# Lightning attention and a Mish layer by seven products: one bank opened earlier, three steps moved up, one sum on GpSimd

## The chip, the cores and the metric

The kernel runs on one core of a Trainium2 chip. The metric is device time in microseconds (us) for one execution. A profile shows one execution: its span is the time from the first to the last instruction, and its own time adds what lies around the span.

## The reference

Two parts, one after the other. First a causal attention with decay: 4 batches, 8 heads, 768 positions, head size 64, with `lam` one decay per head. The reference works in blocks and carries a state:

```
out   = ((q k^T) * D) v + (q * lam^(i+1)) state
state = lam^block * state + (k * lam^(block-1-i))^T v
```

Its output, seen as x of 3072 rows by 512, goes through two matrix products with an activation between them: `h = x @ w_in` (512 to 2048), `g = h * tanh(softplus(h))` (Mish), `out = g @ w_out` (2048 to 512). Inputs and output are float32; the kernel computes in float16 with float32 sums.

## The kernel before

**Tiling.** The positions are cut into six groups (n = 0 to 5) of 128 positions of each of the four batches, so a group has four chunks of 128 tokens, 512 tokens in all, and 24 chunks run through the kernel (group n has chunks 4n to 4n+3). While TensorE does the two layers of group n, the attention of group n+1 is done in between, and the loads of group n+2 are issued. The first layer gives hidden features in 16 tiles of 128; `hsg` holds Mish of them, `xt` the tokens that come in.

**Seven products.** The second layer is computed for 2x2 blocks of tokens and features by seven products instead of eight (P1 to P7, `fast_unit` from L660), which needs sums of quarters of `w_out` (`tsum`, `weight_sum` L452) and of `hsg` (`gsum`, `token_sum` L571). In groups 2 to 5 the last four of the 16 hidden tiles of the first layer are computed in the same way (`set_unit` L506), from sums of `w_in` (`isum`, `in_sum` L472) and of `xt` (`xsum`, `x_sum` L484). There the order is P1, P2, P5, P6, P7, P3, P4. P1 is copied out (`u1`), P2 adds to it in its bank and goes to Mish. P5 is copied to `p5`. P6 adds to P1: ScalarE copies `u1` into the bank of z (L546), and P6's products add to that; ScalarE then copies z into the bank of y (L561). P7 adds to z, P3 to y, and VectorE adds `p5` to both (L542) for Mish.

**Order.** The schedule is written out by hand: each engine runs its instructions in the order in which the program issues them, and waits by semaphores. A list of units (L733 for group 0, L797 for the others) is what TensorE does; after each unit the loop issues what is attached to its number: loads (`slots`, on GpSimd's queue, behind a small `pace` copy), sums, `turn` (scales k, L269, and transposes q and k by DMA on SyncE's queue), and `visit` (attention). In groups 2 to 5, where `d` is 2, units 0 to 3 and 6 to 9 are each two hidden tiles for half of the tokens (`mm1_duo` L422, eight products), unit 4 is P1 and such a tile pair, unit 5 P2 and one, unit 10 P5 and P6, unit 11 a tile pair, unit 12 P7 and P3, unit 13 a tile pair and P4; units 14 to 27 are the second layer.

**Attention in the visits.** `pair_a` (L320) forms k^T v of two chunks (`pv`, L328) in two PSUM banks; VectorE adds the state (`raw`, L288) and scales it (`state`, L293). `pair_s` (L338) forms the scores of two chunks in four banks (L349), the part from the state (L357), and masks the scores on VectorE (`sb`, L365). `pair_o` (L368) applies them to v, scales the result and transposes it into the next `xt`. In group 0 the attention of group 1 goes chunk by chunk: `look_t` (transposes of k and q, `pk` and `pq`, L211), `look_s` (scores, masks L239), `look_kv` and `look_o`. It needs each chunk's scaled k (`ktil`, `scale_k` L262), which VectorE makes, and GpSimd for chunks 6 and 7 (L265).

**Banks.** PSUM has eight banks, given out by tags: `ph` two, `po` two, `pS`, `pk`, `pq`, `pO` one each. A tile with a tag waits until the readers of the tile before in that bank are done. In `set_unit` the tags are set at L532: x (P1, P2) and z (P6, P7, P4) in `po`, w (P5) in `pS`, y (P3) in `pk`. In unit 5 `pair_a` takes both `po` banks; in unit 6 `pair_s` takes `pS`, `pk` and both `po` banks.

**In group 0** units 0 to 15 are the hidden tiles one by one (`mm1_unit` L410), 16 to 19 P1 and P5, 20 to 23 P6 and P2 in halves, 24 to 29 P7, P3, P4. `in_sum` is issued after unit 12, ahead of the `weight_sum` and `token_sum` steps that P5 and P6 read. `weight_sum(3, 1)`, the second half of the sum that P4 reads, is issued after unit 25 on VectorE.

Of the kernel before, what the change touches and what calls it, by code (L numbers as in the profile page):

```python
# [20 lines left out]
def kernel(  # L21
# [10 lines left out]
    nc = tc.nc  # L32
# [7 lines left out]
    NKI = DF // 128  # L40
# [228 lines left out]
    def turn(i):  # L269

        scale_k(i)
        for src, name, to in ((qn, "qraw", qraw), (ktil, "kraw", kraw)):
            to[i] = work.tile([128, JP, C], F16, name=name, tag=name, bufs=4)
            nc.sync.dma_start_transpose(out=to[i], in_=src[i].rearrange("p h c -> p (h c)"))
# [171 lines left out]
    tsum = [const.tile([128, HK, HN], F16, name=f"tsum{i}") for i in range(4)]  # L446
# [2 lines left out]

        return wout[2 * r + s][:, :, c * HN : (c + 1) * HN]  # L450

    def weight_sum(i, s):  # L452

        ks = slice(s * NKI // WS, (s + 1) * NKI // WS)
        a, b, op = (
            (w_quarter(0, 1, s), w_quarter(0, 0, s), ALU.subtract),
            (w_quarter(1, 1, s), tsum[0][:, ks, :], ALU.subtract),
            (w_quarter(1, 1, s), w_quarter(0, 1, s), ALU.subtract),
            (w_quarter(1, 0, s), tsum[1][:, ks, :], ALU.subtract),
        )[i]  # L460
        nc.vector.tensor_tensor(out=tsum[i][:, ks, :], in0=a, in1=b, op=op)  # L461

    KH = NKC // 2
    SU = NKI - 4
# [19 lines left out]
    def x_sum(n, i):  # L484

        xsum[n, i] = work.tile([128, KH, 2 * C], F16, name=f"xsum{i}", tag=f"xsum{i}", bufs=1)
        x = xt[n]
        k0_, k1_ = slice(0, KH), slice(KH, NKC)
        lo, hi = slice(0, 2 * C), slice(2 * C, 4 * C)
        a, b, op = (  # L490
            lambda: (x[:, k0_, hi], x[:, k1_, hi], ALU.add),
            lambda: (xsum[n, 0], x[:, k0_, lo], ALU.subtract),
            lambda: (x[:, k0_, lo], x[:, k0_, hi], ALU.subtract),
            lambda: (x[:, k1_, lo], xsum[n, 1], ALU.subtract),
        )[i]()
        nc.vector.tensor_tensor(out=xsum[n, i], in0=a, in1=b, op=op)
# [9 lines left out]
    def set_unit(n, step):  # L506

        def x_quarter(r, c):
            return lambda kk: xt[n][:, c * KH + kk, r * 2 * C : (r + 1) * 2 * C]

        def x_part(i):
            return lambda kk: xsum[n, i][:, kk, :]

        def w_quarter_(r, c):
            return lambda kk, m: i_quarter(r, c)[:, kk, m * 128 : (m + 1) * 128]

        def w_part_(i):
            return lambda kk, m: isum[i][:, kk, m * 128 : (m + 1) * 128]

        key, lhs, rhs = {  # L520
            "P1": lambda: ("x", w_quarter_(0, 0), x_quarter(0, 0)),
            "P2": lambda: ("x", w_quarter_(1, 0), x_quarter(0, 1)),
            "P6": lambda: ("z", w_part_(1), x_part(1)),
            "P5": lambda: ("w", w_part_(0), x_part(0)),
            "P7": lambda: ("z", w_part_(2), x_part(2)),
            "P3": lambda: ("y", w_quarter_(1, 1), x_part(3)),
            "P4": lambda: ("z", w_part_(3), x_quarter(1, 1)),
        }[step]()

        def place(key):  # L530
            if (n, key) not in first:
                tag, bufs = {"x": ("po", 2), "z": ("po", 2), "w": ("pS", 1), "y": ("pk", 1)}[key]  # L532
                first[n, key] = ps.tile([128, 2, 2 * C], F32, name=f"s{key}", tag=tag, bufs=bufs)
            return first[n, key]

        def kept(key, src, tag, bufs):
            first[n, key] = work.tile([128, 2, 2 * C], F32, name=key, tag=tag, bufs=bufs)
            nc.scalar.activation(first[n, key], src, AF.Copy)  # L538

        def plus_(r, key):  # L540
            o = work.tile([128, 2, 2 * C], F32, name="hs", tag="hs", bufs=2)
            nc.vector.tensor_tensor(out=o, in0=first[n, key], in1=first[n, "p5"], op=ALU.add)  # L542
            return lambda: mish(n, r, 1, o)

        if step == "P6":
            nc.scalar.activation(place("z"), first[n, "u1"], AF.Copy)  # L546
        t = place(key)
        for m in range(2):
            for kk in range(KH):
                nc.tensor.matmul(  # L550
                    t[:, m, :], lhs(kk, m), rhs(kk),
                    start=(step in ("P1", "P5") and m == 0 and kk == 0), stop=(kk == KH - 1),
                    skip_group_check=True)
        if step == "P1":
            kept("u1", t, "osb", 4)
        elif step == "P2":
            mish(n, 0, 0, t)
        elif step == "P5":
            kept("p5", t, "p5", 1)
        elif step == "P6":  # L560
            nc.scalar.activation(place("y"), t, AF.Copy)  # L561
        elif step == "P7":
            plus_(1, "z")()
        elif step == "P3":
            plus_(0, "y")()
        elif step == "P4":
            mish(n, 1, 0, t)
# [165 lines left out]
    units = [(mm1_unit, (0, ni)) for ni in range(NKI)]  # L733
# [4 lines left out]
    for u, (fn, args) in enumerate(units):  # L738
        put_off = []
        fn(*args, **({"then": put_off} if u in (23, 25) else {}))  # L740
        if u < B - 1:
            look_kv(u + 1, "pq" if u == 0 else "po")()
        if 8 <= u < 8 + NVB - B:
            nc.vector.memset(vz[u - 8 + B][:, :, D : 2 * D], 0.0)
        elif u == 13:
            nc.vector.tensor_scalar(out=maskT, in0=rel, scalar1=0.0, scalar2=None, op0=ALU.is_ge)
        for i, s in {14: ((0, 0),), 15: ((0, 1),), 18: ((1, 0), (2, 0)),
                     20: ((1, 1), (2, 1))}.get(u, ()):
            weight_sum(i, s)
        for i, part in sums.get(u, ()):  # L750
            token_sum(0, i, part)
        if u == NKI - 4:
            for i in range(4):
                in_sum(i)
        if u == 22:
            scale_k(4)
            weight_sum(3, 0)
        then = [f(i, "po" if i == 5 else "ph") if f is look_kv else f(i) for f, i in visit.get(u, ())]
        if u == 23:
            scale_k(5)  # L760
            scale_k(6)
        if u == 25:
            weight_sum(3, 1)
        for f in put_off + then:
            if f:
                f()
        if u in (25, 26, 27):
            for _ in range(2):
                ahead.pop(0)()
        if u == 26:  # L770
            scale_k(7)
    next_state(1, 0)

    for n in range(1, NG):
        r, s, t = Pair(), Pair(), Pair()
        r.n, r.bs, s.n, s.bs, t.n, t.bs = n, (2, 3), n + 1, (0, 1), n + 1, (2, 3)
        visit = {}
        d = 0 if n == 1 else 2
        if 1 < n < NG - 1:
            visit[5] = pair_a, r  # L780
        if n < NG - 1:
            visit[6 if d else 11] = pair_s, s
            visit[16 - d] = pair_o, s
# [7 lines left out]
        def duo(g, half):  # L791
            return mm1_duo, (n, g, half * (GT // 2), (half + 1) * (GT // 2))

        def part(step):
            return set_unit, (n, step)

        if d:  # L797
            units = [[duo(g, 0)] for g in range(4)]
            units += [[part("P1"), duo(4, 0)], [part("P2"), duo(5, 0)]]
            units += [[duo(g, 1)] for g in range(4)]  # L800
            units += [[part("P5"), part("P6")], [duo(4, 1)], [part("P7"), part("P3")], [duo(5, 1), part("P4")]]
        else:
            units = [[duo(g, half)] for half in range(2) for g in range(NKI // 2)]
# [14 lines left out]
        for u, calls in enumerate(units):  # L818
            for fn, args in calls:
                fn(*args)  # L820
            if n == 1 and u == 0:
                turn(8)
                look_s(7)
            if n == 1 and u == 2:
                f = look_kv(7)
                look_o(7)
                f()
                next_state(1, 1)
            for _ in range({0: 1, 1: 1, 2: 2, 3: 1, 4: 1}.get(u, 0) if n == 1 else 0):
                pace()  # L830
                ahead.pop(0)()
            if later and u in slots:
                pace()
                later.pop(0)()
            for i, part in sums.get(u, ()):
                token_sum(n, i, part)
            if turns.get(u, NG * B) < NG * B:
                turn(turns[u])
            if u in visit:
                f, s_ = visit[u]  # L840
                s_.spare = ("po", "po") if u < 12 else ("pS", "pk") if f is pair_a else ("ph", "po")
                f(s_)
            if d and u in (6, 8):
                for i in (0, 1) if u == 6 else (2, 3):
                    x_sum(n, i)


# [28 lines left out]
```

## Time and profile before

| | |
|---|---|
| Median of 3 runs | 210.1 us (209.75 to 210.49) |
| Profiled execution, its own time | 209.93 us |
| Its span | 208.2 us |
| Granted TensorE clock, mean | 1.000 |
| VectorE busy | 142.6 us (69%) |
| ScalarE busy | 98.9 us (48%) |
| GpSimd busy | 81.1 us (39%) |

How to read the lines that follow: PE is TensorE (PEld its weight loads), DVE VectorE, ACT ScalarE, POOL GpSimd, SP SyncE; a q behind the name is that engine's queue of instructions. A line names the source line (L550), the operation, and out<-in by the names of the tiles. In the timeline the first two numbers are start and length in us; in brackets stands how long the engine was idle before, and what released it. Products overlap each other, so a length includes the time that a product takes to pass through; the distance between two starts is the better measure. A wait for several semaphores is put down to the one that came last.

### The profile page before, as it was taken

Reading aid. Unit: us, or ns where it says so; the run is one execution under the profiler, and the core shown is the slowest. Engines: PE = TensorE matmul, PEld = TensorE weight load, DVE = VectorE, ACT = ScalarE, POOL = GpSimd, SP = SyncE. Lnnn points to the kernel's source line nnn. Section 1 sums busy time; section 2 is a strip of 40 time slices with the busy share of each in tenths; the row PEclk is TensorE's granted clock in tenths of the full one; section 3 lists DMA queues with packets and bytes.
Section 4 is the critical chain, followed back from the end, with each engine's and each line's share of the span. In section 5 each row is a group of like instructions: output and inputs, shape, how many; then the busy total and the mean of one; then the engine's idle time right before and its main releaser. Section 6 shows DMA issues by size and latency. Waiting matters only on the chain. (4 is left out here: it accounts for less than half of the span.)

```text
span 208.2 us, 5077 instructions
## 1 busy us (share of the span) xinstructions
PE 193.2 (93%) x2065; PEld 158.9 (76%) x2065; DVE 142.6 (69%) x279; ACT 98.9 (48%) x174; POOL 81.1 (39%) x129
## 2 busy tenths in 40 slices
PE   7978998999999999997999997999997999997993
PEld 3645445878888998875998875998875988886883
DVE  7788369799927969384799574799565676322823
ACT  5684663323665421746530646530646630676430
POOL 7994333795678950037751027752000000000000
PEclk9999999999999999999999999999999999999999
DMA  9999999999999999849999759999950023500014
GB/s 131 144 148 197 207 205 188 155 182 201 141 122 181 153 128 231 206 80 92 89 136 214 182 102 82 93 116 211 208 104 8 2 50 104 151 3 0 3 50 153
DMA packets 112459, 26.82 MB, mean 129 GB/s; under 512 B 101555, under 2 KB 112435, under 8 KB 112435
## 3 DMA queue, kind: packets, MB, share of 16 engines
q0 software_dynamic: 77552, 13.37, 88.7%
q1 hardware_dynamic: 30848, 9.97, 26.3%
q10 hardware_dynamic: 4034, 3.15, 5.0%
q8 instruction: 16, 0.26, 0.5%
q14 instruction: 9, 0.07, 0.1%
HBM read 27.26 MB, written 6.29 MB: 161 GB/s over the span
## 5 line engine op out<-in xcount | busy, mean ns | idle before, releaser
L434 PE MATMUL ph<-xt,win 128*128 128x256 f16 x512 | 60.9, 273 | 0.0
L434 PEld LDWEIGHTS <-win 128*128 128x128 f16 x512 | 49.1, 98 | 5.9
L441 ACT ACTIVATE hsg<-ph 128x512 f16<-128x512 f32 x64 | 38.1, 596 | 24.9 <-PE ph L434 24.8
L600 PEld LDWEIGHTS <-gsum 128*128 128x128 f16 x384 | 36.5, 98 | 6.8 <-DVE gsum L586 1.1
L600 PEld LDWEIGHTS <-hsg 128*128 128x128 f16 x272 | 26.0, 98 | 3.3
L586 DVE TENSOR_TENSOR gsum<-hsg 128x1024 f16<-128x1024 f16 x24 | 15.8, 687 | 12.9 <-ACT hsg L441 7.6
L600 PE MATMUL z<-tsum,gsum 128*128 128x256 f16 x192 | 23.3, 273 | 0.6 <-DVE tsum L461 0.6
L600 PE MATMUL x<-wout,hsg 128*128 128x256 f16 x192 | 23.7, 273 | 0.0
L75 POOL DMA_DIRECT2D qn<-in_q_dram x23 | 20.4, 888 | 7.6 <-DMA wout<-in_moe_w_out_dram 3.3
L67 POOL DMA_DIRECT2D kn<-in_k_dram x23 | 20.5, 892 | 6.1 <-DMA win<-in_moe_w_in_dram 2.4
L78 POOL DMA_DIRECT2D vz<-in_v_dram x24 | 21.2, 884 | 4.1 <-DMA wout<-in_moe_w_out_dram 1.7
L396 POOL COPY paced<-hsg 1x1 f16<-1x1 f16 x33 | 8.9, 270 | 34.8 <-ACT hsg L441 33.8
L365 DVE TENSOR_TENSOR sb<-pS,maskT 128x512 f16<-128x512 f32 x32 | 19.9, 682 | 0.9 <-PE pS L349 0.7
L288 DVE TENSOR_TENSOR raw<-pv,state 64x256 f32<-64x256 f32 x24 | 10.1, 422 | 13.5 <-PE pv L328 12.9
L265 DVE TENSOR_TENSOR ktil<-kn,lk 128x512 f16<-128x512 f16 (+1 forms) x22 | 14.6, 684 | 2.4 <-DMA kn<-in_k_dram 2.4
L405 PE MATMUL ph<-xt,win 128*128 128x512 f16 x64 | 14.5, 379 | 0.3 <-ACT xt L257 0.3
L657 ACT ACTIVATE osum<-z 128x512 f32<-128x512 f32 x5 | 3.0, 598 | 23.7 <-PE z L600 23.7
L542 DVE TENSOR_TENSOR hs<-sz,p 128x512 f32<-128x512 f32 x4 | 2.8, 692 | 15.5 <-PE sz L550 15.5
L600 PE MATMUL w<-tsum,gsum 128*128 128x256 f16 x96 | 11.8, 273 | 0.6 <-DVE gsum L586 0.6
L600 PE MATMUL y<-wout,gsum 128*128 128x256 f16 x96 | 12.3, 273 | 0.0
L417 ACT ACTIVATE hsg<-ph 128x512 f16<-128x512 f32 x16 | 9.6, 597 | 5.8 <-PE ph L405 5.8
L550 PEld LDWEIGHTS <-isum 128*128 128x128 f16 x64 | 6.2, 96 | 7.4 <-issue 6.2
(114 smaller groups left out, 271.8 us busy)
## 6 DMA issues: line engine op xcount, KB each, us to landing
vz<-in_v_dram POOLq DMA_DIRECT2D x24, 128.0 KB, 5.5
out_dram<-osum SPq DMA_DIRECT2D x12, 256.0 KB, 3.6
kn<-in_k_dram POOLq DMA_DIRECT2D x23, 128.0 KB, 5.4
qn<-in_q_dram POOLq DMA_DIRECT2D x23, 128.0 KB, 5.3
out_dram<-osum ACTq DMA_DIRECT2D x11, 256.0 KB, 3.9
wout<-in_moe_w_out_dram POOLq DMA_DIRECT2D x4, 512.0 KB, 16.7
win<-in_moe_w_in_dram POOLq DMA_DIRECT2D x3, 512.0 KB, 10.2
win<-in_moe_w_in_dram POOLq DMA_DIRECT2D x2, 256.0 KB, 6.3
```

The lines of the kernel that those rows point to most:

```text
L67: nc.gpsimd.dma_start(out=kn[i], in_=chunk_rows(k, i))
L75: nc.gpsimd.dma_start(out=qn[i], in_=chunk_rows(q, i))
L78: nc.gpsimd.dma_start(out=vz[i % NVB][:, :, 0:D], in_=chunk_rows(v, i))
L265: (nc.gpsimd if B + 1 < i < 2 * B else nc.vector).tensor_tensor(out=t, in0=kn[i], in1=bc(lk, 2, D), op=ALU.mult)
L288: nc.vector.tensor_tensor(out=raw[rs, b % 2, j0 : j0 + nj, :], in0=pv[rs, :, rs], in1=olds(rs), op=ALU.add)
L365: nc.vector.tensor_tensor(out=s.sb[m][t], in0=sc[m][t], in1=bc(maskT, 1, JP), op=ALU.mult)
L405: nc.tensor.matmul(ph_t[ni][:, lo:hi], w_in(ni, kc), xt[n][:, kc, lo:hi], start=(kc == 0), stop=(kc == NKC - 1),)
L417: nc.scalar.activation(hsg[n][:, ni, :], ph_t.pop(ni), AF.Mish)
L434: nc.tensor.matmul(t[:, m, lo - half * h : hi - half * h], w_in(ni, kc), xt[n][:, kc, lo:hi], start=(m == 0 and kc == 0), stop=(kc == NKC ...
L441: nc.scalar.activation(hsg[n][:, 2 * g : 2 * g + 2, half * h : half * h + h], t, AF.Mish)
L586: nc.vector.tensor_tensor(out=gsum[n, i][:, ks, :], in0=a, in1=b, op=op)
L600: nc.tensor.matmul(places(n, key)[:, blk, lo:hi], lhs(kk, blk), rhs(kk, lo, hi), start=(fresh and kk == 0 and blk == 0), stop=(kk == HK - ...
```

## The change

- `set_unit` gets a step `"open"`, which takes the banks of w and z and has ScalarE copy `u1` into z. It is issued at the end of unit 9, after the tile pair; before, the copy was issued in unit 10 behind P5 and its copy to `p5`.
- The bank of x (P1, P2) has the tag `pS` now, that of w (P5) `po`.
- `pair_a` for the second two chunks is visited after unit 3, not 5.
- The first x sum is issued before `pair_s` after unit 6, so ahead of its masks on VectorE; the other three follow the masks. Before, two followed the masks, and two came after unit 8.
- In group 0 the four sums of `w_in` are issued after unit 8, not 12, and `weight_sum(3, 1)` is issued after unit 23 instead of 25, on GpSimd, where it stands between the scaled k of chunk 6 and the loads of group 2.

```diff
-    def weight_sum(i, s):
+    def weight_sum(i, s, engine=None):
...
-        nc.vector.tensor_tensor(out=tsum[i][:, ks, :], in0=a, in1=b, op=op)
+        (engine or nc.vector).tensor_tensor(out=tsum[i][:, ks, :], in0=a, in1=b, op=op)
...
+            "open": lambda: (None,) * 3,
...
-                tag, bufs = {"x": ("po", 2), "z": ("po", 2), "w": ("pS", 1), "y": ("pk", 1)}[key]
+                tag, bufs = {"x": ("pS", 1), "z": ("po", 2), "w": ("po", 2), "y": ("pk", 1)}[key]
...
-        if step == "P6":
+        if step == "open":
+            place("w")
             nc.scalar.activation(place("z"), first[n, "u1"], AF.Copy)
+            return
...
-        if u == NKI - 4:
+        if u == 8:
             for i in range(4):
                 in_sum(i)
...
             scale_k(5)
             scale_k(6)
-        if u == 25:
-            weight_sum(3, 1)
+            weight_sum(3, 1, nc.gpsimd)
...
-            visit[5] = pair_a, r
+            visit[3] = pair_a, r
...
-            units += [[duo(g, 1)] for g in range(4)]
+            units += [[duo(g, 1)] for g in range(3)] + [[duo(3, 1), part("open")]]
...
+            if d and u == 6:
+                x_sum(n, 0)
             if u in visit:
...
-            if d and u in (6, 8):
-                for i in (0, 1) if u == 6 else (2, 3):
+            if d and u == 6:
+                for i in range(1, 4):
                     x_sum(n, i)
```

## The prediction

> **What bounds the kernel now.** I read the page first: TensorE is busy for 93% of the span, so only its gaps can be won. The profiled execution took 209.93 us, its span 208.2 us; 1.73 us lie outside and stay. Then the waits with TensorE as the waiter (columns: total us, times, longest).
>
> ```profile
> span 208.2 us, 5077 instructions
> ...
> PE 193.2 (93%) x2065; PEld 158.9 (76%) x2065; DVE 142.6 (69%) x279; ACT 98.9 (48%) x174; POOL 81.1 (39%) x129
> ```
>
> ```profile
> PE sz L550 <- ACT sz L546: 4.8, 4, 1.2
> ...
> PE pS L349 <- DVE raw L288: 1.1, 3, 0.4
> ...
> PE sw L550 <- DVE xsum L496: 0.7, 3, 0.2
> ...
> PE w L600 <- DVE gsum L586: 0.6, 1, 0.6
> PE z L600 <- DVE tsum L461: 0.6, 1, 0.6
> ...
> PE pk L211 <- DVE sb L239: 0.4, 1, 0.4
> ```
>
> The change aims at all six. The first comes once in each of groups 2 to 5, the next two once in groups 2 to 4, the last three in group 0. These idle times count from a modelled end, so I work with starts below. The timeline of group 2 shows how the first three hang together (start, length, engine, work); groups 3 and 4 have the same waits (three times 0.36 us make the 1.1).
>
> ```profile
> 89.23 1.74 DVE L288 TENSOR_TENSOR raw<-pv,state 64x256 f32<-64x256 f32 x4 [3.98 <-PE pv L328]
> ...
> 90.22 0.45 PE L349 MATMUL pS<-qraw,kraw 64*128 64x128 f16 x9
> ...
> 91.03 0.40 PE L349 MATMUL pS<-qraw,kraw 64*128 64x128 f16 x7 [0.36 <-DVE raw L288]
> ...
> 91.59 2.79 PE L434 MATMUL ph<-xt,win 128*128 128x256 f16 x24
> 91.73 2.48 DVE L365 TENSOR_TENSOR sb<-pS,maskT 128x512 f16<-128x512 f32 x4
> ...
> 94.42 0.60 ACT L441 ACTIVATE hsg<-ph 128x512 f16<-128x512 f32 x1 [0.28 <-PE ph L434]
> ...
> 94.60 0.60 PE L550 MATMUL sw<-xsum,isum 128*128 128x256 f16 x4 [0.22 <-DVE xsum L496]
> ...
> 95.73 0.60 ACT L546 ACTIVATE sz<-u 128x512 f32<-128x512 f32 x1
> ...
> 96.38 0.60 PE L550 MATMUL sz<-xsum,isum 128*128 128x256 f16 x4 [1.18 <-ACT sz L546]
> ```
>
> Nine score products run, then TensorE stops until `raw` has emptied a `po` bank; then 24 hidden products, P5, and a stop until ScalarE has done Mish, p5 and the copy into z, in that order. Two undisturbed cases give the prices: the same scores in group 1, and P6 in group 5, which has no pair work.
>
> ```profile
> 63.88 0.62 PE L349 MATMUL pS<-qraw,kraw 64*128 64x128 f16 x16
> ...
> 64.67 3.67 PE L434 MATMUL ph<-xt,win 128*128 128x256 f16 x32
> ```
>
> ```profile
> 187.16 0.60 ACT L441 ACTIVATE hsg<-ph 128x512 f16<-128x512 f32 x1 [0.28 <-PE ph L434]
> ...
> 187.65 0.59 ACT L538 ACTIVATE p<-sw 128x512 f32<-128x512 f32 x1
> ...
> 188.12 0.61 ACT L546 ACTIVATE sz<-u 128x512 f32<-128x512 f32 x1
> ...
> 188.78 0.60 PE L550 MATMUL sz<-xsum,isum 128*128 128x256 f16 x4 [1.23 <-ACT sz L546]
> ```
>
> **The change, part by part. k^T v two units sooner.** No instruction is added; the eight products move ahead of P1, P2 and two hidden units. `raw` then runs in VectorE's 3.98 us of idle time, and its bank is free when the scores want it. From first score to next hidden product: now 91.59 - 90.22 = 1.37 us; undisturbed 64.67 - 63.88 = 0.79 us. Gain **0.58 us** in groups 2, 3 and 4. If that idle time were missing, the wait would return, no more. The scaling of k and its transposes on SP's queue fall behind `raw`; the scores that use them come in the next half of the group.
>
> **Bank swap and x sum.** P1's bank moves to `pS`, which the scores take next: they now wait for P2's Mish. Two units of eight hidden products (2.79 us for 24, so about 0.9 us each) lie between, against one 0.60 us Mish: nothing. P5's bank moves to `po`, freed by the first two of four masks (2.48 us from 91.73, so by 93.0), well before P5 at 94.60: nothing. The first x sum waits only for the half of xt that the unit ahead of the scores also reads, so it doesn't hold the masks. P5 loses its wait for it; what is late next is ScalarE.
>
> **P6's bank opened a unit ahead.** In the source it is a unit; in ScalarE's queue it is one place: Mish, copy, p5 instead of Mish, p5, copy. So P6 does not become free. ScalarE starts the next operation 187.65 - 187.16 = 0.49 us after a Mish, and P6 starts 188.78 - 188.12 = 0.66 us after the copy: P6 at Mish + 1.15 us. Now it is Mish + 1.96 (96.38 - 94.42) in groups 2 to 4 and + 1.62 (188.78 - 187.16) in group 5. Gain **0.81 us** three times, **0.47 us** once. The copy waits for two masks too, over by then. Of the 4.8 us waited here about 3 should stay, 1.23 - 0.47 = 0.76 each.
>
> **Sums of w_in sooner, in group 0.**
>
> ```profile
> 25.96 0.87 POOL L67 DMA_DIRECT2D kn<-in_k_dram  x1 [1.85 <-DMA win<-in_moe_w_in_dram]
> ...
> 29.12 0.69 DVE L586 TENSOR_TENSOR gsum<-hsg 128x1024 f16<-128x1024 f16 x1 [1.66 <-ACT hsg L417]
> ...
> 31.18 0.42 DVE L480 TENSOR_TENSOR isum<-win 128x512 f16<-128x512 f16 x1
> ...
> 31.94 0.60 ACT L417 ACTIVATE hsg<-ph 128x512 f16<-128x512 f32 x1 [0.27 <-PE ph L405]
> ...
> 32.31 0.42 DVE L480 TENSOR_TENSOR isum<-win,isum 128x512 f16<-128x512 f16 x1
> ...
> 33.52 0.61 PE L600 MATMUL w<-tsum,gsum 128*128 128x256 f16 x4
> ...
> 33.98 0.69 DVE L586 TENSOR_TENSOR gsum<-hsg 128x1024 f16<-128x1024 f16 x1
> ...
> 34.73 1.48 PE L600 MATMUL w<-tsum,gsum 128*128 128x256 f16 x12 [0.60 <-DVE gsum L586]
> ...
> 36.04 0.69 DVE L461 TENSOR_TENSOR tsum<-wout,tsum 128x1024 f16<-128x1024 f16 x1
> ...
> 36.78 1.05 PE L600 MATMUL z<-tsum,gsum 128*128 128x256 f16 x8 [0.57 <-DVE tsum L461]
> ```
>
> Four sums, 31.18 to 32.73, leave VectorE's queue ahead of the gsum that P5 waits for. They go into 1.66 us of idle time before 29.12; their weights landed by 25.96. That gsum can start at 32.7 (its Mish ends at 32.54) instead of 33.98, the tsum for P6 at 36.04 - 1.3 = 34.7, ready at 35.4. P5 runs through; P6 starts about 35.5 instead of 36.78: **1.3 us** sooner. If the idle time were taken, the old wait would stand.
>
> **One sum on GpSimd.** VectorE loses a 0.69 us sum ahead of the masks that `pk` waited for: those **0.4 us** go, so TensorE could reach the last chunk's transposes 1.7 us sooner, at 48.8. But look at GpSimd's queue.
>
> ```profile
> 33.57 0.87 POOL L67 DMA_DIRECT2D kn<-in_k_dram  x1 [1.67 <-DMA wout<-in_moe_w_out_dram]
> ```
>
> ```profile
> kn<-in_k_dram POOLq DMA_DIRECT2D x1, 128.0 KB, 8.2
> ```
>
> ```profile
> 41.54 0.68 DVE L265 TENSOR_TENSOR ktil<-kn,lk 128x512 f16<-128x512 f16 x1
> ...
> 41.93 1.20 POOL L265 TENSOR_TENSOR ktil<-kn,lk 128x512 f16<-128x512 f16 x1 [1.43 <-ACT osum L639]
> ...
> 43.08 0.95 POOL L67 DMA_DIRECT2D kn<-in_k_dram  x1
> ...
> 46.64 1.09 POOL L265 TENSOR_TENSOR ktil<-kn,lk 128x512 f16<-128x512 f16 x1
> ...
> 50.51 0.39 PE L211 MATMUL pk<-ident,ktil 128*128 128x128 f16 x4
> ```
>
> The sum goes in at 43.08. Behind it stand four load issues and chunk 7's scaled k (46.64), all back to back, and that k is what the transposes at 50.51 read. The first scaled k can't come forward: its load lands 33.57 + 8.2 = 41.8. The sum has no row on GpSimd. Nearest: a 512-element product there, 1.09 to 1.20 us. Low end 1.09 (length without price), high end 2 x 1.20 = 2.4 and, if something holds it up for one 0.69 us VectorE operation, 3.1. I take 2 x 1.09 = 2.2 us. Then the scaled k runs from 48.84 to 49.93 and `pk` starts at 49.98 at best, 1.1 us after TensorE is ready: of the 1.7 us only 50.51 - 49.98 = **0.53 us** stay. The four loads behind the sum come 2.2 us later too; what they bring is read only after the transposes at 50.51. P4 reads the sum itself: its two units of eight products, about 0.9 us each, stand ahead of `pk`, so it starts near 47, and the sum is done by 45.3.
>
> What speaks against this part is the port that both engines read through. The row: with VectorE's product on two SBUF tensors running until 42.22, GpSimd's took 1.20 us instead of 1.09. The Trainium skill (SBUF — State Buffer, Who interferes with whom) says that a VectorE instruction with two SBUF inputs and a GpSimd instruction that reads SBUF exclude each other, and that the loser "fully blocks". By that rule the product would have ended at 42.22 + 1.09 = 43.31; the next issue started at 43.08, so this trace shows less than the rule. Meeting one such operation would make the sum 2.3 us by the row and up to 2.9 by the rule, 0.1 to 0.7 us on the total. The VectorE work that stands beside the sum (masks, P7's addition, `raw`) reads PSUM, so the forecast adds nothing.
>
> **Sum.** 3 x (0.58 + 0.81) + 0.47 + 0.53 = 5.17 us. 209.93 - 5.17 = 204.8 us. The median of the three runs shown, 210.1, is 0.17 higher, well inside their spread of 0.74.
>
> **Rivals.** *GpSimd's sum is hidden* (about 1.1 us): chunk 7's k is ready at 48.9 and group 0 keeps 1.6 instead of 0.53: 203.7 us. For it: both inputs are plain f16. Against: a sum of 1024 elements would then take no longer than a product of 512.
>
> *The sum is held longer*: 3 to 4.2 us, by the port or its operands, each us one us for TensorE: 205.6 to 206.8 us. At 4 us P4 waits too, but ahead of the same place.
>
> *The opening opens nothing*: ScalarE stands at the copy until the masks free the `po` bank, and P6 keeps its distance. Without the 0.81 and 0.47: 204.8 + 2.9 = 207.7; with half, 206.2. Against: VectorE's chain before the masks gets shorter, not longer.
>
> *P6 wholly free*: the 0.76 us left four times go as well: 204.8 - 3.0 = 201.8. The queue order speaks against it.
>
> *Slower than before*: only a GpSimd sum long enough to hold TensorE for all that the groups gain. `pk` starts at 47.78 + d for a sum of d us; the gain is 4.64 + 50.51 - 47.78 - d, zero at d = 7.4 us. At 9 us the kernel takes 211.6. A product of half the length takes 1.2 us here, so it needs six times that for twice the work.
>
> **How the numbers follow.** Forecast 0.55 (204.2 to 205.5, with d from 1.6 to 2.9 us); sum hidden 0.12; sum held 0.12; opening nothing 0.11, most of it partly; P6 free 0.03; slower 0.07. The range runs from the hidden sum, with 0.4 us of slack, to the held one: 203.3 to 206.9, leaving out P6 free, slower, and part of the opening case, under 0.2. Within 0.3%, about what a measurement of this kernel can tell from no change, lies only the edge of the long sum: faster 0.91, same 0.02, slower 0.07.
>
> **What would show it.** TensorE's waits: no `pS` on `raw`, no `sw` on `xsum`, no `w` on `gsum`; `sz` on the copy, four times, about 0.76 us each; P6 1.15 us after its Mish; scores to hidden product 0.79 us. New: `pk` waiting about 1 us for GpSimd's `ktil` near 50 us, behind a sum of about 2.2 us. I am wrong if that sum is far from 2.2, if ScalarE's copy starts later than 0.5 us after the Mish, or if a load shows up as a wait of TensorE.

## The result and the profile after

Six runs of the changed kernel took 204.8 to 206.21 us, median 205.16; six of the kernel before, on the same chip, 209.64 to 211.03, median 210.3. The ratio is 0.977 (95% interval 0.973 to 0.980): 5.1 us less, where 5.17 were forecast. The execution that was profiled was the slowest of the six, 206.21 us. In the changed kernel the lines behind the edits are 1 to 3 higher: L600 is L603, L586 is L589, L550 is L553, L546 is L548, L538 is L539.

The head of the page, then TensorE's waits (total us, times, longest):

```profile
span 204.4 us, 5076 instructions
...
PE 191.2 (94%) x2065; PEld 158.2 (77%) x2065; DVE 141.8 (69%) x278; ACT 99.0 (48%) x174; POOL 82.2 (40%) x130
```

```profile
PE sz L553 <- ACT sz L548: 3.0, 4, 0.7
PE pk L211 <- POOL ktil L265: 1.5, 1, 1.5
PE ph L434 <- DMA xt<-xtok: 1.2, 1, 1.2
```

The waits for `raw`, `xsum`, `gsum` and `tsum` are gone. The wait for the copy has shrunk from 4.8 to 3.0, and `pk` waits for GpSimd now: both as forecast, though the second is 1.5 us where about 1 was named. The third line was not in the sum: a wait for a transfer, once, in group 2. The timeline of group 2 (start, length, engine, work, idle before) has it beside the three gains:

```profile
86.15 1.75 DVE L288 TENSOR_TENSOR raw<-pv,state 64x256 f32<-64x256 f32 x4 [1.94 <-PE pv L328]
...
90.18 1.03 PE L434 MATMUL ph<-xt,win 128*128 128x256 f16 x8 [1.19 <-DMA xt<-xtok]
91.14 0.62 PE L349 MATMUL pS<-qraw,kraw 64*128 64x128 f16 x16
...
91.93 2.79 PE L434 MATMUL ph<-xt,win 128*128 128x256 f16 x24
...
94.56 0.60 PE L553 MATMUL sw<-xsum,isum 128*128 128x256 f16 x4
94.76 0.60 ACT L441 ACTIVATE hsg<-ph 128x512 f16<-128x512 f32 x1 [0.28 <-PE ph L434]
...
95.25 0.60 ACT L548 ACTIVATE sz<-u 128x512 f32<-128x512 f32 x1
95.77 0.59 ACT L539 ACTIVATE p<-sw 128x512 f32<-128x512 f32 x1
95.90 0.60 PE L553 MATMUL sz<-xsum,isum 128*128 128x256 f16 x4 [0.74 <-ACT sz L548]
```

`raw` starts three microseconds earlier in the span than it did (89.23 before), and all 16 score products run in one piece: 91.93 - 91.14 = 0.79 us to the next hidden product. The copy now stands between the Mish and p5, and P6 starts 95.90 - 94.76 = 1.14 us after the Mish. In group 0:

```profile
27.47 0.42 DVE L480 TENSOR_TENSOR isum<-win,isum 128x512 f16<-128x512 f16 x1
...
32.42 0.69 DVE L589 TENSOR_TENSOR gsum<-hsg 128x1024 f16<-128x1024 f16 x1
...
33.34 1.91 PE L603 MATMUL w<-tsum,gsum 128*128 128x256 f16 x16
...
35.22 1.05 PE L603 MATMUL z<-tsum,gsum 128*128 128x256 f16 x8
...
42.29 1.04 POOL L265 TENSOR_TENSOR ktil<-kn,lk 128x512 f16<-128x512 f16 x1 [1.36 <-PE pv L302]
...
43.30 2.12 POOL L461 TENSOR_TENSOR tsum<-wout,tsum 128x1024 f16<-128x1024 f16 x1
...
45.37 0.95 POOL L67 DMA_DIRECT2D kn<-in_k_dram  x1
...
48.93 1.08 POOL L265 TENSOR_TENSOR ktil<-kn,lk 128x512 f16<-128x512 f16 x1
...
50.07 0.40 PE L211 MATMUL pk<-ident,ktil 128*128 128x128 f16 x4 [1.50 <-POOL ktil L265]
```

P5 runs its 16 products without a stop, and P6 starts at 35.22 instead of 36.78. From P5's start that is 1.88 us instead of 3.26: 1.38 sooner, where 1.3 was forecast. Fifteen microseconds later little of that is left: behind a GpSimd sum of 2.12 us come the loads and chunk 7's k, and `pk` starts at 50.07 instead of 50.51, 0.44 us sooner.

With these sizes the sum closes to a tenth. The forecast span is 208.2 - 5.17 = 203.03; `pk` gained 0.09 us less than forecast, and the transfer cost 1.19: 204.31, and the profile has 204.4.

### The profile page after: what moved, and what is told of

The parts are those of the page before. It is cut to its first block, busy times and chain, and to the rows that moved or that the text cites. A ratio compares the mean times of both kernels' runs of the same rounds, so it can differ in the third digit from the quotient of the medians.

```text
span 204.4 us, 5076 instructions
## 1 busy us (share of the span) xinstructions
PE 191.2 (94%) x2065; PEld 158.2 (77%) x2065; DVE 141.8 (69%) x278; ACT 99.0 (48%) x174; POOL 82.2 (40%) x130
## 5 line engine op out<-in xcount | busy, mean ns | idle before, releaser
L434 PEld LDWEIGHTS <-win 128*128 128x128 f16 x512 | 49.2, 98 | 7.3 <-DMA xt<-xtok 1.4
L603 PEld LDWEIGHTS <-gsum 128*128 128x128 f16 x384 | 36.7, 98 | 5.1 <-DVE gsum L589 0.3
L603 PEld LDWEIGHTS <-hsg 128*128 128x128 f16 x272 | 26.1, 98 | 3.2
L603 PE MATMUL x<-wout,hsg 128*128 128x256 f16 x192 | 23.7, 273 | 0.0
L589 DVE TENSOR_TENSOR gsum<-hsg 128x1024 f16<-128x1024 f16 x24 | 15.8, 686 | 11.0 <-ACT hsg L441 7.2
L603 PE MATMUL z<-tsum,gsum 128*128 128x256 f16 x192 | 23.3, 273 | 0.0
L396 POOL COPY paced<-hsg 1x1 f16<-1x1 f16 x33 | 7.7, 235 | 31.0 <-ACT hsg L441 29.9
L603 PE MATMUL y<-wout,gsum 128*128 128x256 f16 x96 | 12.3, 273 | 0.0
L405 PEld LDWEIGHTS <-win 128*128 128x128 f16 x64 | 6.1, 98 | 7.8 <-DMA win<-in_moe_w_in_dram 1.2
L603 PE MATMUL w<-tsum,gsum 128*128 128x256 f16 x96 | 11.6, 273 | 0.0
```

The source lines that it names most:

```text
L405: nc.tensor.matmul(ph_t[ni][:, lo:hi], w_in(ni, kc), xt[n][:, kc, lo:hi], start=(kc == 0), stop=(kc == NKC - 1),)
L434: nc.tensor.matmul(t[:, m, lo - half * h : hi - half * h], w_in(ni, kc), xt[n][:, kc, lo:hi], start=(m == 0 and kc == 0), stop=(kc == NKC ...
L589: nc.vector.tensor_tensor(out=gsum[n, i][:, ks, :], in0=a, in1=b, op=op)
L603: nc.tensor.matmul(places(n, key)[:, blk, lo:hi], lhs(kk, blk), rhs(kk, lo, hi), start=(fresh and kk == 0 and blk == 0), stop=(kk == HK - ...
```

## The experiments

The theory is the prediction's: the gains of groups 2 to 5 are real and stay, while GpSimd's sum eats most of what group 0 gains. The rival is that the sum is hidden, or that the gain comes from other parts than those named. Each edit is shown against the changed kernel, that of e11 against the kernel before. The kernel before was run again beside each set, on the same chip; its medians there were 209.62 (e1 to e4), 209.49 (e7 to e10) and 209.57 us (e5, e6, e11 and the repeat). So kernels of different sets are compared by ratios; half a per cent is about 1 us. Each row stands for 4 to 6 executions, that of e11 for 12.

| kernel | median us | lowest to highest | ratio to before | 95% interval |
|---|---|---|---|---|
| changed | 205.16 | 204.8 to 206.21 | 0.9766 | 0.9733 to 0.9799 |
| changed, again | 205.02 | 204.42 to 205.82 | 0.9780 | 0.9749 to 0.9810 |
| e1 sum on VectorE after unit 25 | 204.02 | 203.86 to 204.46 | 0.9722 | 0.9694 to 0.9750 |
| e2 chunk 7's k ahead of the loads | 206.84 | 205.57 to 208.29 | 0.9858 | 0.9814 to 0.9901 |
| e3 sums of w_in late | 204.70 | 204.18 to 204.84 | 0.9749 | 0.9720 to 0.9777 |
| e4 bank opened behind p5 | 206.52 | 206.4 to 206.89 | 0.9843 | 0.9815 to 0.9871 |
| e5 k^T v late | 206.72 | 206.31 to 207.73 | 0.9859 | 0.9827 to 0.9892 |
| e6 x sum behind masks | 205.13 | 204.66 to 206.14 | 0.9785 | 0.9755 to 0.9814 |
| e7 copy ahead of the last Mish | 202.04 | 201.51 to 202.51 | 0.9635 | 0.9620 to 0.9649 |
| e8 e7 and e9 together | 200.48 | 200.03 to 200.79 | 0.9568 | 0.9552 to 0.9585 |
| e9 sum on VectorE after unit 22 | 203.76 | 202.53 to 204.1 | 0.9714 | 0.9692 to 0.9736 |
| e10 e9, sums of w_in late | 204.97 | 204.12 to 207.15 | 0.9797 | 0.9756 to 0.9838 |
| e11 group 0's edits alone | 209.44 | 208.52 to 210.1 | 0.9982 | 0.9963 to 1.0001 |

The traces hold a finer measure for groups 2 to 4: the distance from P5 of one group to P5 of the next, which came out the same, to 0.01 us, from group 2 to 3 and from 3 to 4. It is 31.70 us in the kernel before and in e11, and 30.30 in the changed kernel, in both of its profiles: 1.40 us less, where 0.58 + 0.81 = 1.39 was forecast. In e4 it is 30.79, in e5 30.89, in e6 30.30 and in e7 29.60.

### The repeat: whose is the wait for xt?

The changed kernel once more.

> The changed kernel once more, beside these runs. Theory (the wait of group 2 for xt, 1.2 us in the first profile, belongs to that execution, since the loads behind the GpSimd sum land late by a varying amount): around 205 us, and a profile without that wait is as likely as one with it. Rival (the wait belongs to the kernel): 1 us or more of waiting for xt in this profile too.

Its profile has a span of 202.9 us and no wait for xt. One row of SyncE's queue, in the timeline of the changed kernel's first profile and then of the repeat:

```profile
82.98 4.29 SPq L386 DMA_TRANSPOSE xt<-xtok  x2
```

```profile
82.81 2.88 SPq L386 DMA_TRANSPOSE xt<-xtok  x2
```

And the transposes of k between 58 and 83 us, from the view of the DMA issues (kind, count, median us from issue to landing), in the same order:

```profile
kraw<-ktil SPq DMA_TRANSPOSE x4, 7.9
```

```profile
kraw<-ktil SPq DMA_TRANSPOSE x4, 6.1
```

The same program issues two transposes of xt in 4.29 or in 2.88 us, and its other transposes land in 7.9 or 6.1. So the 1.2 us belong to that execution, and not to every execution of the changed kernel; whether the change makes such executions more frequent, two profiles can't show. 208.2 - 202.9 = 5.3 us is the difference between two undelayed profiles, beside 5.17 forecast. Why the transfers were slow in that execution is open; e10 below met it too (a wait of 0.9 us for xt), and its GpSimd does not make the sum.

### e4 and e7: the order of ScalarE's queue

e4 keeps the swapped banks, but issues the copy behind p5 again.

```diff
-            units += [[duo(g, 1)] for g in range(3)] + [[duo(3, 1), part("open")]]
-            units += [[part("P5"), part("P6")], [duo(4, 1)], [part("P7"), part("P3")], [duo(5, 1), part("P4")]]
+            units += [[duo(g, 1)] for g in range(3)] + [[duo(3, 1)]]
+            units += [[part("P5"), part("open"), part("P6")], [duo(4, 1)], [part("P7"), part("P3")], [duo(5, 1), part("P4")]]
```

> The changed kernel, with the copy into the bank of z back in unit 10 behind the copy to p5; banks as changed. Theory (opening it a unit ahead is worth one place in ScalarE's queue): P6 1.62 instead of 1.15 us after its Mish in groups 2 to 5, 4 x 0.47 = 1.9 us more, about 207.1 us; the wait of sz four times near 1.2 us again. Rival (the copy's place does not matter, the gain of the groups came from the scores and the x sum alone): no change, 205.2 us.

TensorE's wait for the copy in e4:

```profile
PE sz L553 <- ACT sz L548: 4.9, 4, 1.2
```

The old wait is back, 1.9 us more than with the copy in unit 9, and each group is 0.49 us longer. The time rose by 1.3 to 1.6 us by the ratios; the intervals hold the 1.9 too. "The opening opens nothing" falls. e7 goes the other way and puts the copy ahead of the tile pair, so that in ScalarE's queue it passes the last Mish as well:

```diff
-            units += [[duo(g, 1)] for g in range(3)] + [[duo(3, 1), part("open")]]
+            units += [[duo(g, 1)] for g in range(3)] + [[part("open"), duo(3, 1)]]
```

> The changed kernel, with the copy into the bank of z issued in unit 9 ahead of the tile pair instead of behind it, so ahead of that pair's Mish on ScalarE. Theory (what is left of the wait of P6, 4 x 0.74 us, is ScalarE's order Mish, copy): P6 follows P5 without a wait; then P7 waits for ScalarE's copy of z into y, so 0.75 us less in each of groups 2 to 5, 3.0 us less than the changed kernel: about 202.2 us. Rival (the copy then stands at the masks that free the bank, and Mish behind it): the wait of sz stays near 0.7 us, 205.2 us or more.

The timeline of e7 in group 2:

```profile
93.47 0.60 ACT L548 ACTIVATE sz<-u 128x512 f32<-128x512 f32 x1
...
93.64 0.60 PE L553 MATMUL sw<-xsum,isum 128*128 128x256 f16 x4
93.98 0.59 ACT L441 ACTIVATE hsg<-ph 128x512 f16<-128x512 f32 x1
94.11 0.60 PE L553 MATMUL sz<-xsum,isum 128*128 128x256 f16 x4
94.46 0.60 ACT L539 ACTIVATE p<-sw 128x512 f32<-128x512 f32 x1
```

P6 follows P5 after 0.47 us (1.34 in the changed kernel) and the wait for the copy is gone from the list, all 3.0 us of it. The time falls by 1.4% to 202.04 us: 2.8 us. The prediction's rival "P6 wholly free" priced this rightly; the change just doesn't do it, because one Mish still stands ahead of the copy.

### e5 and e6: k^T v and the x sum

e5 visits `pair_a` after unit 5 again, e6 issues all four x sums behind the masks.

```diff
-            visit[3] = pair_a, r
+            visit[5] = pair_a, r
```

```diff
-            if d and u == 6:
-                x_sum(n, 0)
...
-                for i in range(1, 4):
+                for i in range(4):
                     x_sum(n, i)
```

> The changed kernel, with k^T v of the second two chunks back after unit 5. Theory: the scores stop again until raw has emptied a bank, 0.58 us in each of groups 2, 3 and 4, 1.7 us more than the changed kernel: about 206.9 us; the wait of pS on raw is there three times. Rival (what is late in these groups is ScalarE before P6 anyway, and hides it): no change, 205.2 us.

> The changed kernel, with the first x sum back behind the masks. Theory (once the bank of P6 is what is late, the x sums have room: the first would end about 0.4 us after where the second is needed least, and P6 starts 0.5 us behind that): no change beyond 0.3 us, 205.2; P5 waits 0.1 to 0.3 us, and P6's wait shrinks by as much. Rival (the x sum is worth its 0.2 us three times): 0.6 us more, 205.8 us.

e5, TensorE's waits:

```profile
PE sz L553 <- DVE xsum L496: 2.2, 3, 0.7
...
PE pS L349 <- DVE raw L288: 1.1, 3, 0.4
```

The stop in the scores is back, each of these groups is 0.59 us longer, and the kernel takes 1.70 us more than the repeat on the same chip; 3 x 0.58 = 1.74 was the forecast. That P6 now waits for an x sum in the list costs nothing: in all four groups of e5 it still starts 1.14 us after the Mish and 0.65 after the copy, so the sum ended with the copy.

e6 shows no such price: 205.13 beside 205.02. Its P5 and P6 in group 2, and then a row of the kernel before:

```profile
93.58 0.60 PE L553 MATMUL sw<-xsum,isum 128*128 128x256 f16 x4
...
94.81 0.60 PE L553 MATMUL sz<-xsum,isum 128*128 128x256 f16 x4 [0.64 <-ACT sz L548]
```

```profile
95.23 0.60 ACT L538 ACTIVATE p<-sw 128x512 f32<-128x512 f32 x1 [0.21 <-PE sw L550]
```

P5 starts 0.11 us later (1.23 us ahead of P6, not 1.34), and P6 waits 0.64 instead of 0.74; P6 keeps its 1.14 us after the Mish. In the kernel before, ScalarE stood 0.21 us until P5 was done, and the copy stood behind p5, so a late P5 made P6 late. Now the copy stands ahead of p5, and the 0.11 us are lost in P6's own wait. This reading rests on the order and these rows; no run takes back the copy and the x sum together and leaves the rest.

### e1, e2 and e9: what GpSimd's sum costs

e1 gives the sum back to VectorE at its old place, e9 to VectorE after unit 22.

```diff
-            weight_sum(3, 1, nc.gpsimd)
+        if u == 25:
+            weight_sum(3, 1)
```

```diff
         if u == 22:
             weight_sum(3, 0)
+            weight_sum(3, 1)
...
-            weight_sum(3, 1, nc.gpsimd)
```

> The changed kernel, with the moved sum back on VectorE after unit 25; all else as changed. Theory (chunk 7's scaled k stands behind the GpSimd sum, and TensorE waits for it: 50.07 instead of 47.52 + 0.87 = 48.4): the wait of pk on GpSimd's ktil goes, the old wait of pk on VectorE's masks (0.4 to 0.6 us) comes back, so pk of chunk 7 near 49.0 and 1.1 us less than the changed kernel: about 204.1 us. Rival (the sum on GpSimd is a gain, since it relieves VectorE): 0.4 to 0.6 us more, about 205.7 us.

> The changed kernel, with the moved sum on VectorE after unit 22 instead of GpSimd; the scaled k of chunk 7 and the loads get back their places in GpSimd's queue. Theory (the sum on GpSimd costs by the queue behind it, both by chunk 7's k and by late loads; on VectorE it cost by standing ahead of masks): neither the wait of pk on ktil nor that on masks, 1.7 us less than the changed kernel: about 203.5 us, and no wait on a DMA in groups 1 and 2. Rival (VectorE has no room anywhere in group 0): the wait of pk or of P7 on VectorE comes back, 204.0 us or more.

e1 in two views, its waits and its timeline:

```profile
PE pk L211 <- DVE sb L239: 1.0, 1, 1.0
```

```profile
42.45 1.04 POOL L265 TENSOR_TENSOR ktil<-kn,lk 128x512 f16<-128x512 f16 x1 [1.48 <-PE pv L302]
42.74 1.29 DVE L461 TENSOR_TENSOR tsum<-wout,tsum 128x1024 f16<-128x1024 f16 x1
...
49.70 0.39 PE L211 MATMUL pk<-ident,ktil 128*128 128x128 f16 x4
```

Chunk 7's `pk` no longer waits, and starts at 49.70; near 49.0 was expected. The time falls to 0.972 of before, about 1.0 us below the changed kernel. The traces show only part of that: counted from P5's start, `pk` comes after 16.23 us, beside 16.73 and 16.82 in the two profiles of the changed kernel, so 0.5 to 0.6 us sooner. Where the rest of the 1.0 lies isn't shown. Still, the sum is not hidden on GpSimd; moving it there costs more than the mask wait that it was to remove.

In e9 the sum runs on VectorE right behind its first half, at 39.3 us; there is no wait for `pk` at all, it comes 15.79 us after P5, and the time is 203.76 us, between the theory's 203.5 and the rival's 204.0. One wait on VectorE is there, 0.57 us of P6's second half at 37.60, for another sum, whose weights landed late:

```profile
36.86 0.69 DVE L461 TENSOR_TENSOR tsum<-wout,tsum 128x1024 f16<-128x1024 f16 x1 [1.21 <-DMA wout<-in_moe_w_out_dram]
```

e2 leaves the sum on GpSimd and moves chunk 7's scaled k ahead of the loads, so that only the loads wait for it.

```diff
+        if u == 25:
+            scale_k(7)
...
-        if u == 26:
-            scale_k(7)
```

> The changed kernel, with chunk 7's scaled k issued on GpSimd right behind the sum, ahead of the four load issues. Theory (that queue place is what TensorE waits for): the k runs 45.4 to 46.5, pk of chunk 7 starts at 48.4 without a wait, 1.6 us less: about 203.6 us. Rival (the loads of chunks 8 and 9, now 1.1 us later still, become the wait in group 1): pk starts early, but TensorE or VectorE waits for kn or xt in groups 1 and 2, and the time stays at 205.2 or more.

The timeline of e2, in group 0 and in group 1:

```profile
45.87 1.04 POOL L265 TENSOR_TENSOR ktil<-kn,lk 128x512 f16<-128x512 f16 x1
...
46.86 0.95 POOL L67 DMA_DIRECT2D kn<-in_k_dram  x1
...
49.03 0.39 PE L211 MATMUL pk<-ident,ktil 128*128 128x128 f16 x4
...
52.44 0.88 POOL L67 DMA_DIRECT2D kn<-in_k_dram  x1
...
61.42 0.69 DVE L265 TENSOR_TENSOR ktil<-kn,lk 128x512 f16<-128x512 f16 x1 [4.29 <-DMA kn<-in_k_dram]
...
65.58 0.40 PE L349 MATMUL pS<-qraw,kraw 64*128 64x128 f16 x8 [2.78 <-DMA kraw<-ktil]
```

`pk` runs at 49.03 without a wait, and yet the kernel is slower than the changed one, by 0.8%. The loads behind the sum go out from 46.86 on (43.08 before, 45.37 after the change); in group 1 VectorE waits 4.29 us for a load of k, the transposes of k follow late, and the scores wait 2.78 us. The theory's 203.6 us failed, and the time and the waits are those of its rival.

The rival's reason, the loads of chunks 8 and 9 going out later still, is not what the trace shows: VectorE scales their k at 51.77 and 53.69 without waiting for a load. The k that it waits for is chunk 11's, and that goes out in group 1, at 52.44; in the repeat it goes out at 53.32, later. There it landed 6.1 us after its issue and VectorE waited 2.05 us (2.37 in the kernel before); in e2 it took 9.0 us. So this transfer was slow, not late. All six executions of e2 took 205.57 us or more, so it is hardly the luck of one. A possible cause that no run tests is that the loads now stand closer together: from chunk 8's k to chunk 11's are 5.58 us in e2 and 8.13 in the repeat.

### e3 and e10: sums of w_in

Both issue the four sums after unit 12 again; e10 does so on top of e9.

```diff
-        if u == 8:
+        if u == NKI - 4:
             for i in range(4):
                 in_sum(i)
```

> The changed kernel, with the four sums of w_in back after unit 12. Theory (the gain of 1.3 us is made ahead of a wait for GpSimd that swallows it; that wait has 1.7 us of room): P6 of group 0 starts 1.3 us later again, pk of chunk 7 still at 50.1, its wait shrinks from 1.5 to about 0.2 us, and the time stays within 0.3 us of the changed kernel, 205.2. Rival (the parts add up): 1.3 us more, about 206.5 us.

> The kernel with the moved sum on VectorE after unit 22, and the four sums of w_in back after unit 12. Theory (with the wait for GpSimd gone, the 1.3 us of the sums of w_in are no longer masked): 1.3 us more than with the early sums, about 204.8 us. Rival (the sums of w_in are worth nothing, whatever stands behind them): no difference, about 203.5 us.

The waits of e3, then those of e10:

```profile
PE pk L211 <- POOL ktil L265: 0.6, 1, 0.6
PE w L603 <- DVE gsum L589: 0.6, 1, 0.6
PE z L603 <- DVE tsum L461: 0.6, 1, 0.6
```

```profile
PE w L603 <- DVE gsum L589: 0.6, 1, 0.6
PE z L603 <- DVE tsum L461: 0.6, 1, 0.6
```

In both the two stops of the kernel before are back. In e3 the wait for GpSimd's k shrinks from 1.5 to 0.6 in return, and the time is that of the changed kernel (204.70): what one stop loses, the next one had been losing anyway. Without that next wait the same edit costs 1.2 us by the medians (e10 beside e9, intervals apart). The size is rough: e10's executions lie 3.0 us apart, and the one profiled met slow transfers. In the traces P6 starts 3.26 us after P5 in e10 and 1.88 in e9, so the prediction's 1.3 us were there. They don't outlast a later wait that ends at a time of its own, and in e9 0.57 of them went to the late weights.

### e11: group 0's edits alone

The kernel before with the edits of group 0 (`in_sum` after unit 8, `weight_sum(3, 1)` on GpSimd after unit 23) and nothing else.

> The kernel before with only the two edits of group 0: the sums of w_in after unit 8, and the moved sum on GpSimd. Theory (1.7 us won, all but 0.5 lost again to chunk 7's scaled k behind the sum, at 50.0 to 50.1): 0.3 to 0.6 us less than before, about 209.3 us where before stands at 209.7. Rival (the two edits keep their 1.7 us): about 208.0 us.

TensorE's waits in e11:

```profile
PE sz L553 <- ACT sz L548: 4.8, 4, 1.2
PE pk L211 <- POOL ktil L265: 1.5, 1, 1.5
...
PE pS L349 <- DVE raw L288: 1.1, 3, 0.4
```

The waits of groups 2 to 5 are those of the kernel before, to within 0.1 us, and the one on GpSimd is there. 209.44 us beside 209.57, 0 to 0.8 us of gain by the interval. Groups 2 to 5 hold the rest, 209.44 - 205.02 = 4.4 us, where the sum had 4.64.

### e8: both improvements

> The changed kernel, with the moved sum on VectorE after unit 22, where VectorE was idle, and the copy into z ahead of the tile pair as in the run of that alone. Both effects, 1.7 and 3.0 us, if they add: about 200.5 us. Rival (the faster groups meet transposes or loads that land late): a wait of TensorE for xt or kraw appears, 201.5 us or more.

e8 joins e7 and e9, and is the fastest of all: 200.48 us, 0.957 of before (0.955 to 0.959). It is 1.56 us below e7 and 3.28 below e9 on the same chip, about what each part gives alone: they add up. When chunk 7's transposes start in e8:

```profile
48.79 0.39 PE L211 MATMUL pk<-ident,ktil 128*128 128x128 f16 x4
```

That is 1.72 us sooner than in the kernel before; the prediction said that TensorE could be there at 48.8. Not all of that need be the edits': P5 already started 0.25 us sooner in this execution, and counted from P5 the gain is 1.47 us (15.52 instead of 16.99), with 0.29 us lost to weights that landed late.

## Why the prediction was right

**The bound, and the six waits.** Right: four are gone, the one for the copy keeps 3.0 us, and `pk` waits for GpSimd instead of the masks. The 0.4 us of the mask wait are not the price of that sum at any time, though: in e1 it comes back with 1.0 us.

**Scores, 3 x 0.58.** Right in size (0.79 us to the hidden product) and in cause: undoing it costs 0.59 us in each group of e5, and 1.70 us in its time.

**P6 at the Mish + 1.15.** Right: 1.14, four times, and 3.0 us of wait kept. The step that read the place in the queue from two undisturbed rows, instead of taking "a unit ahead" at its word, carries the forecast: with P6 free it would have been 201.8, and e7, where P6 is free, took 202.04.

**x sum.** P5's wait for it is gone, and the edit that was given the credit does end the last 0.11 us of it, but that is worth nothing: e6 without that edit has the same time. By the rows above, what freed P6 from a late P5 is the copy's new place ahead of p5. Cause wrong, size right, since the price was booked with P6 as a whole.

**w_in and GpSimd's sum, 0.53 left of 1.7.** Right: 2.12 us for the sum where 2.2 were taken; `pk` kept 0.44 us in the first profile, 0.61 in the repeat (49.90) and 0.28 in e11 (50.23), whose time shows nothing measurable. The cost of the sum, 1.1 us in the rival "hidden", is 0.9 to 1.3 us by `pk` counted from P5 in e9 and e8, where the sum is off GpSimd and costs no wait of its own. That the later loads cost nothing ("what they bring is read only after the transposes at 50.51") no run contradicts: the slow load of e2 is not one of those four.

**The sum.** 204.8 forecast, 205.16 and 205.02 measured. The wait for a transfer, named as a sign of being wrong, did appear, in one of the changed kernel's two profiles; why it came is open.

## What to carry to other kernels

Look at the place in each engine's queue, not at the unit in the source: one position on ScalarE was worth 1.9 us here by the waits, and one more 3.0. An operation that moves to an idle engine is paid by whoever stands behind it there; on a queue that also issues loads they are delayed as well (2.29 us here), and an order that looks better for one (e2) can be worse for the whole. A gain ahead of a wait that ends at a time of its own is lost up to that wait, so take the later wait away first.

## What was not expected of the hardware

In e1 a VectorE sum of 1024 elements took 1.29 us, where the other sums of that line take 0.69 or less. It is the second row of e1's timeline: it starts at 42.74, while GpSimd's product (42.45 to 43.49) is running, and it is 0.60 us longer than the others; GpSimd's product kept its 1.04 us. The prediction weighed such a meeting with GpSimd as the one that is held up; here GpSimd was first, and VectorE paid. The 0.60 us fit the mask wait of 1.0 us in e1 beside 0.4 in the kernel before, where GpSimd only issued loads beside the sum (44.17 to 44.85), and the sum took 0.68. The Trainium skill (SBUF — State Buffer, Who interferes with whom) says that whichever of the two issues first has the shared ports for the whole instruction, and that the other one waits. This row agrees, nearly: 43.49 + 0.69 would be 44.18, and it ended at 42.74 + 1.29 = 44.03. In the changed kernel itself GpSimd's sum met VectorE work that reads PSUM, and took 2.12 us, twice the 1.04 of half the length.
